# Two gated layers on one core: chunk loop outside or slice loop outside

## The chip, the cores and the metric

The kernel runs on one core of a Trainium2 chip. The metric is the time of one execution in microseconds (us), as the device measures it; the engines named below are PE (matrix products), DVE (vector), ACT (activations), POOL (a second elementwise engine) and SP (which issues the transfers). Less is better.

## The reference

The first part is an attention over 16 heads (batch 2, 8 heads, 768 positions, 64 wide) in which a query sees only the keys of its own hash bucket. Its output is 1536 tokens of 512 values, and two layers follow:

```
gate = 1.0 / (1.0 + np.exp(-(x @ w_gate)))     # 512 x 1536
val = x @ w_val                                # 512 x 1536
x = gate * val @ w_out                         # 1536 x 512
h = x @ w_in                                   # 512 x 2048
g = h * np.cos(h)
return (g @ w_out).astype(np.float32)          # 2048 x 512
```

## The kernel before

The weights come from memory as 64-bit floats. `load_raw` brings one block (128 of the 512 rows' columns, or 128 rows of 512; 512 KB) into one of three raw buffers, on SP's queue. `convert` makes 32-bit floats of it: one copy on ACT (line 150, tile `wp`) and three operations on DVE (lines 152, 155 and 169; tiles `wl`, then `w_g`, `w_v`, `w_o`, `w_i`, `w_z`). Every operand of a product is split in a high and a low part (`split`, lines 122 and 123: a cast on ACT, a subtraction on DVE or POOL), and each product is three matmuls: high by high, high by low, low by high.

The tokens are in three chunks of 512 (`xy[c]`, high and low). The inner dimension is cut in slices of 128: 12 in layer 1 (weights g, v, o), 16 in layer 2 (weights i, z). For a chunk and a slice, layer 1 does 24 matmuls in (`glu_in`) and 12 out (`layer_out1`); layer 2 does 12 in (`cos_in`) and 12 out (`layer_out2`). The inner values (`g`) go from PSUM over ACT and DVE into the buffer, are split (`gh`, `gl`), and the out matmuls add them up in four PSUM banks `a`, which are free again after a chunk.

The loop over chunks is outside:

```
units = [(1, c, f) for c in range(NC) for f in range(F1)]
units += [(2, c, f) for c in range(NC) for f in range(F2)]
```

so all weights of a layer are converted during one chunk (those of layer 1 in its first chunk, those of layer 2 during the last chunk of layer 1) and stay in the buffer as 32-bit values; the split of a weight is made anew for each chunk, 204 times in all, nearly always with POOL for the low part. There are 68 conversions. Six weights are converted already during the end of the attention.

The attention's order is written by hand. The order of the two layers on each engine's queue is made by a planner from the program text: it takes what its own clock holds to be ready, the earlier text first. An engine then works its queue strictly in that order. The last pair of heads writes the last 128 of the 512 rows of `xy[1]` and `xy[2]` (lines 454, 470 and 474); `xy[0]` is finished long before.

Of the kernel before, what the change touches and what calls it, by code (L numbers as in the profile page):

```python
# [9 lines left out]
F32 = mybir.dt.float32  # L10
F32R = mybir.dt.float32r
# [7 lines left out]
P = 128  # L19
# [20 lines left out]
def lsh_attention_glu_moe_cos_moe(  # L40
# [32 lines left out]
    OLAG = 2  # L73
    AHEAD = 9
    NFRONT = 6
# [54 lines left out]
    def load_raw(key):  # L130
        nm, f = key
# [12 lines left out]
    def convert(key):  # L144
        nm, f = key
# [17 lines left out]
        slot = order.index(key) % (3 * F1)  # L163
        if slot < NEARLY:
            w = wraw.tile([P, 512], F32, tag="we", name=f"w_{nm}{f}", bufs=NEARLY)
        else:
            pool = wf["front" if slot < NEARLY + NFRONT else "back"]
            w = pool.tile([P, 512], F32, tag="w", name=f"w_{nm}{f}")
# [10 lines left out]
    def keys(l, f):  # L179
        return [(n, f) for n in (("g", "v", "o") if l == 1 else ("i", "z"))]  # L180
# [6 lines left out]
    wf = {}  # L187

# [420 lines left out]
    def moe():  # L609
        with ExitStack() as st:  # L610
            wsp = st.enter_context(tc.tile_pool(name="wsp", bufs=2))
            wk = st.enter_context(tc.tile_pool(name="wk", bufs=2))
            wf["front"] = st.enter_context(tc.tile_pool(name="wff", bufs=NFRONT))
            wk2 = st.enter_context(tc.tile_pool(name="wk2", bufs=2))
            wf["back"] = st.enter_context(
                tc.tile_pool(name="wfb", bufs=3 * F1 - NEARLY - NFRONT)
            )
# [5 lines left out]
            def l_first(key):  # L623
                return key in (("g", 0), ("g", 1), ("v", 1))

            def wsplit(c, key):
                nm, f = key
                h = wsp.tile([P, KT, P], F32R, tag=ROLE[nm] + "h", name=f"{nm}h{c}_{f}")
                lw = wsp.tile([P, KT, P], F32R, tag=ROLE[nm] + "l", name=f"{nm}l{c}_{f}")
                sub = nc.vector if c == 0 and l_first(key) else nc.gpsimd  # L630
                split(h, lw, wt[key].rearrange("p (k c) -> p k c", k=KT), sub)
                ws[c, key] = (h, lw)

            def proj_in(ps, c, key):
                wh, wl = ws.pop((c, key))
# [8 lines left out]
            def gsplit(nm, g):  # L644
                gh = wk.tile([P, 512], F32R, tag="gh", name=f"gh{nm}", bufs=4)
                gl = wk.tile([P, 512], F32R, tag="gl", name=f"gl{nm}", bufs=4)
                split(gh, gl, g, nc.vector)
                return gh, gl

            def glu_in(c, f):  # L650
                pg = ps_h.tile([P, 512], F32, tag="h", name=f"pg{c}_{f}")
                pv_ = ps_h.tile([P, 512], F32, tag="h", name=f"pv{c}_{f}")
                proj_in(pg, c, ("g", f))
                proj_in(pv_, c, ("v", f))
                sg = wk.tile([P, 512], F32, tag="n", name=f"sg{c}_{f}")
                nc.scalar.activation(sg, pg, AF.Sigmoid)  # L656
                g = wk.tile([P, 512], F32, tag="g", name=f"g{c}_{f}")
                nc.vector.tensor_tensor(out=g, in0=pv_, in1=sg, op=ALU.mult)  # L658
                return gsplit(f"1_{c}_{f}", g)

            def cos_in(c, f):
                ph = ps_h.tile([P, 512], F32, tag="h", name=f"ph{c}_{f}")
                proj_in(ph, c, ("i", f))
# [9 lines left out]
                g = wk.tile([P, 512], F32, tag="g", name=f"g2{c}_{f}")  # L673
                nc.vector.tensor_tensor(out=g, in0=ph, in1=r, op=ALU.mult)
                return gsplit(f"2_{c}_{f}", g)
# [3 lines left out]
            def layer_out1(c, f, g):  # L679
                gh, gl = g  # L680
                wh, wl = ws.pop((c, ("o", f)))
                for e in range(KT):
                    if f == 0:
                        acc[e] = ps_a.tile([P, 512], F32, tag=f"a{e}", name=f"a1_{c}_{e}")
                    n = 0
                    for w, m in ((wh, gh), (wh, gl), (wl, gh)):
                        nc.tensor.matmul(  # L687
                            acc[e],
# [6 lines left out]
                    if f == F1 - 1:  # L695
                        nc.scalar.copy(xy[c][:, 0, e, :], acc[e])
                        nc.vector.tensor_tensor(
                            out=xy[c][:, 1, e, :],
                            in0=acc[e],
# [4 lines left out]
            def layer_out2(c, f, g):  # L704
                gh, gl = g
                wh, wl = ws.pop((c, ("z", f)))
                wh, wl = (x.rearrange("p k c -> p (k c)") for x in (wh, wl))
                for t in range(4):
                    if f == 0:
                        acc[t] = ps_a.tile([P, 512], F32, tag=f"a{t}", name=f"a2_{c}_{t}")  # L710
                    n = 0
                    ts = slice(t * P, (t + 1) * P)
                    for m, w in ((gh, wh), (gh, wl), (gl, wh)):
                        nc.tensor.matmul(  # L714
                            acc[t],
# [6 lines left out]
                    if f == F2 - 1:  # L722
                        o = wk2.tile([P, 512], F32, tag="o", name=f"o{c}_{t}", bufs=4)
                        (nc.scalar.copy if t % 2 else nc.vector.tensor_copy)(o, acc[t])
# [5 lines left out]
            units = [(1, c, f) for c in range(NC) for f in range(F1)]  # L730
            units += [(2, c, f) for c in range(NC) for f in range(F2)]

            def wsplit_for(n):
                if n < len(units):
                    l, c, f = units[n]
                    for nm in "gv" if l == 1 else "i":
                        wsplit(c, (nm, f))
                if n >= OLAG:
                    l, c, f = units[n - OLAG]
                    wsplit(c, ("o" if l == 1 else "z", f))  # L740

            pend = []
            convert_to(2 * OLAG)
            wsplit_for(0)
            for n, u in enumerate(units):
                l, c, f = u
                if l == 1:
                    if c == 0:
                        convert_to(min(3 * f + AHEAD, 3 * F1))
                    elif c == NC - 1:  # L750
                        convert_to(3 * F1 + 2 + 3 * max(0, f - 3))
                else:
                    if c == 0:
# [3 lines left out]
                if len(pend) > 2 and n != len(units) - 2:  # L757
                    (l0, c0, f0), g = pend.pop(0)
                    (layer_out1 if l0 == 1 else layer_out2)(c0, f0, g)
            wsplit_for(len(units) + 1)  # L760
            for (l0, c0, f0), g in pend:
                layer_out2(c0, f0, g)
# [44 lines left out]
```

## Time and profile before

| | |
|---|---|
| median of 3 runs | 850.98 us (847.41 to 854.46) |
| profiled execution | 848.18 us, of which the span 846.4 us |
| PE busy | 804.8 us (95%) |
| DVE, ACT, POOL busy | 594.3, 517.1, 471.5 us |
| mean granted clock of PE | 0.990 |

The span runs from the first to the last instruction; 1.8 us of the execution lie around it. Matmuls overlap in the records (each takes 0.39 us, one starts every 0.23 us), so a busy PE isn't always one at its full rate. In lists of waits, the engine and the tile that waited stand first, and then what released them.

### The profile page before, as it was taken

The numbers are of one execution on the slowest core, as the hardware profiler recorded it, in microseconds if no ns is written. First come the engines' busy times: TensorE is split into PE (matmuls) and PEld (weight loads), VectorE is DVE, ScalarE is ACT, GpSimd is POOL, SyncE is SP. The second block draws the span as 40 slices with busy tenths as digits, with TensorE's granted clock in tenths as the row PEclk, the third lists the DMA queues.
The fourth block names the chain that finished last, engine by engine and source line by source line (L and its number), as shares of the span: only waits on it lengthen the run. The fifth ranks groups of instructions, "written<-read, shape, count | busy, mean of one in ns | idle before, by whom it ended". The sixth has DMA issues, their size and how long they took to land.

```text
span 846.4 us, 12255 instructions
## 1 busy us (share of the span) xinstructions
PE 804.8 (95%) x3984; PEld 675.4 (80%) x3984; DVE 594.3 (70%) x1069; ACT 517.1 (61%) x973; POOL 471.5 (56%) x431
## 2 busy tenths in 40 slices
PE   3999999999989998899999999889999999999998
PEld 2798898898988775678888877678888888888886
DVE  4899999999999999933123797775554554455553
ACT  2798898988997454554334454447555655555553
POOL 1779788879853644474444443446444444444441
PEclk8899999999999999999999999999999999999999
DMA  8665665665524456510001354520000100000001
GB/s 197 161 154 137 150 168 139 161 169 136 137 94 141 157 165 187 189 35 1 1 0 50 125 165 142 167 74 1 1 1 0 50 2 0 1 23 28 0 1 50
DMA packets 65455, 75.38 MB, mean 89 GB/s; under 512 B 29168, under 2 KB 51696, under 8 KB 65392
## 3 DMA queue, kind: packets, MB, share of 16 engines
q1 hardware_dynamic: 65392, 74.60, 31.8%
q8 instruction: 32, 0.52, 0.3%
q14 instruction: 31, 0.25, 0.1%
HBM read 45.09 MB, written 3.15 MB: 57 GB/s over the span
## 4 chain that ended last, share of the span: by engine, by line
PE 64%; DVE 13%; issue 7%; DMA 6%; POOL 4%; ACT 4%; SPq 1%; POOLq 0%; DVEq 0%; ACTq 0%
PE a L714 15%; PE ph L639 15%; PE a L687 7%; PE pv L639 6%; PE pg L639 6%; PE t L411 4%; DVE pl L421 2%; PE s L359 2%; PE s L362 2%; PE o L432 2%; PE o L431 2%; DMA raw_z<-in_moe_w_out 2%; POOL p L402 1%; DMA raw_o<-in_moe_w_out 1%; POOL gl L123 1%
## 5 line engine op out<-in xcount | busy, mean ns | idle before, releaser
L123 DVE TENSOR_TENSOR gl<-g,gh 128x512 fp32r<-128x512 f32 x84 | 94.4, 1124 | 44.8 <-ACT gh L122 44.7
L639 PE MATMUL ph<-xy,ih 128*128 128x512 f32 x384 | 118.2, 389 | 0.0
L123 POOL TENSOR_TENSOR zl<-w_z,zh 128x512 fp32r<-128x512 f32 x48 | 62.1, 1293 | 86.2 <-ACT zh L122 83.8
L385 ACT ACTIVATE p<-s,cb 128x768 f32<-128x768 f32 x96 | 96.0, 1000 | 20.3 <-DVE cb L371 13.9
L411 PE MATMUL t<-ident,p 128*128 128x128 f32 x576 | 95.1, 273 | 3.3 <-DVE pl L421 2.3
L639 PE MATMUL pv<-xy,vh 128*128 128x512 f32 x288 | 90.8, 396 | 7.8 <-DVE g L658 4.8
L421 DVE TENSOR_TENSOR pl<-t,ph 128x384 fp32r<-128x384 f32 x192 | 96.9, 540 | 1.7 <-ACT ph L416 0.4
L416 ACT CAST ph<-t 128x384 fp32r<-128x384 f32 x192 | 90.7, 484 | 11.9 <-PE t L411 8.7
L402 POOL TENSOR_SCALAR p<-p,r 128x768 f32<-128x768 f32 x96 | 86.8, 908 | 15.4 <-DVE r L398 8.4
L366 DVE TENSOR_REDUCE mm<-s 128x1 f32<-128x768 f32 x96 | 90.6, 944 | 5.2 <-PE s L362 5.2
L123 POOL TENSOR_TENSOR il<-w_i,ih 128x512 fp32r<-128x512 f32 x48 | 62.1, 1295 | 53.1 <-ACT ih L122 53.1
L639 PE MATMUL pg<-xy,gh 128*128 128x512 f32 x288 | 89.8, 391 | 1.4 <-ACT sg L656 1.2
L411 PEld LDWEIGHTS t<-ident,p 128*128 128x128 f32 x576 | 73.7, 141 | 15.1 <-DVE pl L421 7.1
L639 PEld LDWEIGHTS ph<-xy,ih 128*128 128x128 f32 x384 | 72.1, 188 | 15.0
L123 POOL TENSOR_TENSOR ol<-w_o,oh 128x512 fp32r<-128x512 f32 x36 | 51.3, 1425 | 55.0 <-ACT oh L122 52.6
L431 PE MATMUL o<-ph,vs 128*128 128x384 f32 x192 | 80.4, 419 | 1.3 <-ACT e L440 1.3
L123 POOL TENSOR_TENSOR vl<-w_v,vh 128x512 fp32r<-128x512 f32 x35 | 50.0, 1428 | 55.2 <-ACT vh L122 48.1
L123 POOL TENSOR_TENSOR gl<-w_g,gh 128x512 fp32r<-128x512 f32 x34 | 48.8, 1437 | 55.4 <-ACT gh L122 50.7
L359 PE MATMUL s<-k,q 96*128 96x384 f32 x192 | 69.9, 364 | 10.1 <-DMA k<-bf 8.4
L714 PE MATMUL a<-zh,gh 128*128 128x512 f32 x192 | 74.7, 389 | 0.0
L639 PE MATMUL ph<-xy,il 128*128 128x512 f32 x192 | 74.7, 389 | 0.0
L714 PE MATMUL a<-zl,gh 128*128 128x512 f32 x192 | 74.7, 389 | 0.0
(106 smaller groups left out, 1957.9 us busy)
## 6 DMA issues: line engine op xcount, KB each, us to landing
q<-x SPq DMA_DIRECT2D x47, 192.0 KB, 3.3
k<-x SPq DMA_DIRECT2D x47, 192.0 KB, 3.6
raw_i<-in_moe_w_in SPq DMA_DIRECT2D x16, 512.0 KB, 3.8
raw_z<-in_moe_w_out SPq DMA_DIRECT2D x16, 512.0 KB, 3.2
raw_g<-in_moe_w_gate SPq DMA_DIRECT2D x12, 512.0 KB, 3.8
raw_v<-in_moe_w_val SPq DMA_DIRECT2D x12, 512.0 KB, 3.7
raw_o<-in_moe_w_out SPq DMA_DIRECT2D x12, 512.0 KB, 3.3
nv<-in_v SPq DMA_DIRECT2D x8, 384.0 KB, 3.5
```

What stands on the lines that cost most here:

```text
L123: sub.tensor_tensor(out=dst_l, in0=src, in1=dst_h.bitcast(F32), op=ALU.subtract)
L359: nc.tensor.matmul(o, hh["q2"][0:96, t, :], hh["k2"][0:96, sl, :], start=True, stop=False)
L366: nc.vector.tensor_reduce(mm[:, g % NM, 1:2], s_t[g], axis=AX.XY, op=ALU.min)
L385: nc.scalar.activation(pt, s_t.pop(g), AF.Exp, bias=cb[:, 1:2], scale=cb[:, 0:1], accum_out=sm)
L402: nc.gpsimd.tensor_scalar(out=pt, in0=pt, scalar1=r_t.pop(g), scalar2=1.0, op0=ALU.mult, op1=ALU.mult)
L411: nc.tensor.transpose(pt[:, i, :], pv_[:, j * P : (j + 1) * P], ident)
L416: nc.scalar.copy(ph, pt_t[w])
L421: nc.vector.tensor_tensor(out=pl, in0=pt_t.pop(w), in1=ph_t[w].bitcast(F32), op=ALU.subtract)
L431: nc.tensor.matmul(o_t[u], vs[:, j, :], ph_t.pop(w), start=(j == 0), stop=False)
L639: nc.tensor.matmul(ps, w[:, kt, :], xy[c][:, hl, kt, :], start=(n == 0), stop=(n == 11))
L687: nc.tensor.matmul(acc[e], w[:, e, :], m, start=(f == 0 and n == 0), stop=(f == F1 - 1 and n == 2),)
L714: nc.tensor.matmul(acc[t], m[:, ts], w, start=(f == 0 and n == 0), stop=(f == F2 - 1 and n == 2),)
```

## The change

In both layers the loop over slices is outside and the three chunks inside. A new list `items` gives the order: for each slice the in matmuls of chunks 1, 2 and 3 and the out matmuls of chunk 1; the out matmuls of chunks 2 and 3 follow after the last slice, slice by slice, the last two slices of chunk 2 ahead of those of chunk 3. The inner values of chunks 2 and 3 stay unsplit in 32 new buffers (`gsp`) until then. The first two slices are mixed so that chunk 1 comes first. Chunk 2 adds up in the four banks of `ps_h`, in which the in products stand else.

A weight is split once and serves all chunks, and its converted form is given back at once; the pools that held a whole layer's weights go, and six buffers (`we`) are left. The out weights (o, z) are loaded, converted and split a second time for the out matmuls of chunks 2 and 3. So there are 96 conversions and loads instead of 68, and 96 splits of weights instead of 204. The number of matmuls (2448) and of inner values' splits (84) is the same.

```diff
-    order = []
-    for f in range(F1 + OLAG):
-        order += [(nm, f) for nm in "gv" if f < F1] + [("o", f - OLAG)] * (f >= OLAG)
-    order += [kk for f in range(F2) for kk in keys(2, f)]
+    def layer_items(l, F):
+        items = [("in", l, 0, 0), ("in", l, 1, 0), ("in", l, 0, 1), ("in", l, 0, 2), ("in", l, 1, 1)]
+        items += [("out", l, 0, 0), ("in", l, 1, 2), ("out", l, 1, 0)]
+        for f in range(2, F):
+            items += [("in", l, f, c) for c in range(NC)] + [("out", l, f, 0)]
+        for f in range(F - 2):
+            items += [("out", l, f, c) for c in range(1, NC)]
+        items += [("out", l, f, c) for c in range(1, NC) for f in (F - 2, F - 1)]
+        return items
+    items = layer_items(1, F1) + layer_items(2, F2)
+    def weights_of(item):
+        kind, l, f, c = item
+        if kind == "in":
+            return [(nm, f, 0) for nm in ("gv" if l == 1 else "i")]
+        return [("o" if l == 1 else "z", f, int(c > 0))]
+    order = list(dict.fromkeys(kk for it in items for kk in weights_of(it)))
...
+            gsp = st.enter_context(tc.tile_pool(name="gsp", bufs=(NC - 1) * F2))
...
+            def gtile(l, f, c):
+                if c == 0:
+                    return wk.tile([P, 512], F32, tag="g", name=f"g{l}_{c}_{f}")
+                return gsp.tile([P, 512], F32, tag="gs", name=f"g{l}_{c}_{f}")
...
+            def acc_tile(l, c, e):
+                if c == 1:
+                    return ps_h.tile([P, 512], F32, tag="h", name=f"a{l}_{c}_{e}")
+                return ps_a.tile([P, 512], F32, tag=f"a{e}", name=f"a{l}_{c}_{e}")
...
+            def ready_to(key):
+                nonlocal ready
+                while ready <= order.index(key):
+                    convert_to(ready + 1)
+                    wsplit(order[ready])
+                    ready += 1
+                    convert_to(min(ready + NEARLY - 2, len(order)))
+            for key in weights_of(items[0]):
+                ready_to(key)
+            for n, (kind, l, f, c) in enumerate(items):
+                late = kind == "out" and c > 0
+                for it in items[n + 1 : n + (3 if late else 4)]:
+                    for key in weights_of(it):
+                        ready_to(key)
+                for it in items[n + 1 : n + 3]:
+                    if it[0] == "out" and it[1:] in gf:
+                        gsplit(*it[1:])
+                if kind == "in":
+                    (glu_in if l == 1 else cos_in)(c, f)
                 else:
-                    if c == 0:
-                        convert_to(3 * F1 + 2 * (f + 3))
-                wsplit_for(n + 1)
-                pend.append((u, glu_in(c, f) if l == 1 else cos_in(c, f)))
+                    (layer_out1 if l == 1 else layer_out2)(c, f)
```

## Rows read from the trace of the kernel before

**Rows 1.** The page: engines' busy time, and busy tenths in 40 slices.
```profile
PE 804.8 (95%) x3984; PEld 675.4 (80%) x3984; DVE 594.3 (70%) x1069; ACT 517.1 (61%) x973; POOL 471.5 (56%) x431
...
PE   3999999999989998899999999889999999999998
...
DVE  4899999999999999933123797775554554455553
```

**Rows 2.** Busy time by stretch: PE, PEld, DVE, ACT, POOL, clock, DMA share, GB/s.
```profile
600.00:830.00 230.00, 230.00 (x1017) 190.44 (x1016) 118.42 (x132) 131.97 (x215) 108.68 (x84) 1.00 0.03 10
470.00:570.00 100.00, 93.14 (x394) 73.71 (x393) 80.82 (x106) 45.25 (x80) 44.81 (x30) 0.98 0.44 138
290.00:369.00 79.00, 70.06 (x288) 52.19 (x288) 72.88 (x94) 40.93 (x71) 36.91 (x26) 1.00 0.55 171
369.00:450.00 81.00, 81.00 (x359) 67.08 (x358) 19.29 (x26) 32.55 (x56) 43.54 (x34) 1.00 0.00 1
```

**Rows 3.** The chain in order of time, its last piece: start, length, what.
```profile
831.66 10.89 PE a L714 x48
```

**Rows 4.** List of waits, 470 to 570 us: total, times, longest.
```profile
ACT wp_z L150 <- DMA raw_z<-in_moe_w_out: 21.2, 12, 4.3
...
POOL vl L123 <- ACT vh L122: 20.0, 7, 6.3
```

**Rows 5.** Timeline of ACT, 518 to 570 us: start, length, instruction, idle before.
```profile
547.95 0.68 ACT L150 ACTIVATE wp_z<-raw_z 128x512 f32<-128x512 f32 x1 [3.28 <-DMA raw_z<-in_moe_w_out]
548.52 0.62 ACT L122 CAST vh<-w_v 128x512 fp32r<-128x512 f32 x1
```

**Rows 6.** Timeline of PE, 518 to 570 us.
```profile
549.19 0.73 PE L639 MATMUL pv<-xy,vh 128*128 128x512 f32 x2 [1.69 <-ACT vh L122]
```

**Rows 7.** DVE's groups by line, 470 to 570 us: busy, mean ns, idle before.
```profile
L155 DVE SCALAR_TENSOR_TENSOR wl_i<-wp_i,wl_i 128x512 int32<-128x512 int32 x13 | 14.2, 1091 | 1.1 <-ACT wp_i L150 0.6
L155 DVE SCALAR_TENSOR_TENSOR wl_z<-wp_z,wl_z 128x512 int32<-128x512 int32 x14 | 13.4, 958 | 0.6
L169 DVE SCALAR_TENSOR_TENSOR w_i<-raw_i,wl_i 128x512 int32<-128x512 int32 x14 | 11.7, 835 | 4.1 <-POOL gl L123 2.8 <-POOL vl L123 1.2
L169 DVE SCALAR_TENSOR_TENSOR w_z<-raw_z,wl_z 128x512 int32<-128x512 int32 x14 | 10.7, 762 | 5.7 <-POOL gl L123 3.3 <-POOL vl L123 2.3
L152 DVE TENSOR_SCALAR wl_z<-raw_z 128x512 int32<-128x512 int32 x14 | 9.8, 702 | 3.0 <-DMA raw_z<-in_moe_w_out 2.9
L123 DVE TENSOR_TENSOR gl<-g,gh 128x512 fp32r<-128x512 f32 x10 | 9.0, 903 | 0.1
L152 DVE TENSOR_SCALAR wl_i<-raw_i 128x512 int32<-128x512 int32 x13 | 8.2, 628 | 4.4 <-DMA raw_i<-in_moe_w_in 4.3
```

**Rows 8.** Groups by line, whole span: DVE's work on layer 2's inner values, POOL's split.
```profile
L123 POOL TENSOR_TENSOR zl<-w_z,zh 128x512 fp32r<-128x512 f32 x48 | 62.1, 1293 | 86.2 <-ACT zh L122 83.8 <-DVE xy L697 2.4
...
L674 DVE TENSOR_TENSOR g<-ph,r 128x512 f32<-128x512 f32 x48 | 33.2, 691 | 35.6 <-ACT r L672 35.6
L669 DVE SCALAR_TENSOR_TENSOR r<-ph,n 128x512 f32<-128x512 f32 x48 | 33.2, 691 | 53.6 <-ACT n L667 53.6
```

**Rows 9.** Timeline of DVE around one operation of POOL, 517 to 520 us.
```profile
517.62 0.41 DVE L152 TENSOR_SCALAR wl_i<-raw_i 128x512 int32<-128x512 int32 x1
...
518.55 0.68 DVE L123 TENSOR_TENSOR gl<-g,gh 128x512 fp32r<-128x512 f32 x1
519.15 1.78 DVE L155 SCALAR_TENSOR_TENSOR wl_i<-wp_i,wl_i 128x512 int32<-128x512 int32 x1
```

**Rows 10.** The same stretch on POOL.
```profile
518.95 1.43 POOL L123 TENSOR_TENSOR ol<-w_o,oh 128x512 fp32r<-128x512 f32 x1 [2.40 <-ACT oh L122]
```

**Rows 11.** DMA issues of the page: number, KB each, us from issue to landing.
```profile
raw_z<-in_moe_w_out SPq DMA_DIRECT2D x16, 512.0 KB, 3.2
```

**Rows 12.** Timeline of PE at the attention's end: first matmuls of layer 1's second slice.
```profile
266.95 0.62 PE L639 MATMUL pg<-xy,gh 128*128 128x512 f32 x2
```

**Rows 13.** Timeline of POOL at the attention's end: the last rows of chunks 2 and 3.
```profile
275.37 1.33 POOL L123 TENSOR_TENSOR gl<-w_g,gh 128x512 fp32r<-128x512 f32 x1 [1.31 <-ACT gh L122]
276.67 2.30 POOL L454 TENSOR_TENSOR ef<-e,ef 128x768 f32<-128x768 f32 x1
279.48 2.70 POOL L474 TENSOR_TENSOR xy<-ef,xy 128x256 fp32r<-128x256 f32 x2 [0.52 <-ACT xy L470]
```

More of the change, by code (lines that the diff above doesn't have):

```diff
@@ L144, in convert @@
     def convert(key):
-        nm, f = key
+        nm, f, _ = key
         rw = raws.pop(key)
@@ L162, in convert @@
         )
[L163 to L168, printed above, removed]
+        w = wraw.tile([P, 512], F32, tag="we", name=f"w_{nm}{f}", bufs=NEARLY)
         nc.vector.scalar_tensor_tensor(
@@ L177, in convert @@
         wt[key] = w
-    def keys(l, f):
-        return [(n, f) for n in (("g", "v", "o") if l == 1 else ("i", "z"))]
-    order = []
-    for f in range(F1 + OLAG):
-        order += [(nm, f) for nm in "gv" if f < F1] + [("o", f - OLAG)] * (f >= OLAG)
-    order += [kk for f in range(F2) for kk in keys(2, f)]
+    def layer_items(l, F):
[7 more added lines that the diff above has]
+        return items
+    assert NC == 3
+    items = layer_items(1, F1) + layer_items(2, F2)
[5 more added lines that the diff above has]
+    order = list(dict.fromkeys(kk for it in items for kk in weights_of(it)))
     done = 0
-    wf = {}
     def convert_to(n):
@@ L621, in moe, with wsplit @@
             ws = {}
[L623 to L632, printed above, removed]
+            def wsplit(key):
+                nm, f, again = key
+                h = wsp.tile([P, KT, P], F32R, tag=ROLE[nm] + "h", name=f"{nm}h{again}_{f}")
+                lw = wsp.tile([P, KT, P], F32R, tag=ROLE[nm] + "l", name=f"{nm}l{again}_{f}")
+                sub = nc.vector if key in (("g", 0, 0), ("g", 1, 0), ("v", 1, 0)) else nc.gpsimd
+                split(h, lw, wt.pop(key).rearrange("p (k c) -> p k c", k=KT), sub)
+                ws[key] = (h, lw)
             def proj_in(ps, c, key):
-                wh, wl = ws.pop((c, key))
+                wh, wl = ws[key]
                 n = 0
@@ L642, in proj_in, with gsplit @@
                         n += 1
[L644 to L648, printed above, removed]
+            def gtile(l, f, c):
+                if c == 0:
+                    return wk.tile([P, 512], F32, tag="g", name=f"g{l}_{c}_{f}")
+                return gsp.tile([P, 512], F32, tag="gs", name=f"g{l}_{c}_{f}")
+            gf, gs = {}, {}
+            def gsplit(l, f, c):
+                gh = wk.tile([P, 512], F32R, tag="gh", name=f"gh{l}_{c}_{f}", bufs=4)
+                gl = wk.tile([P, 512], F32R, tag="gl", name=f"gl{l}_{c}_{f}", bufs=4)
+                split(gh, gl, gf.pop((l, f, c)), nc.vector)
+                gs[l, f, c] = gh, gl
             def glu_in(c, f):
@@ L695, in layer_out1 @@
                     if f == F1 - 1:
-                        nc.scalar.copy(xy[c][:, 0, e, :], acc[e])
+                        nc.scalar.copy(xy[c][:, 0, e, :], acc[c, e])
                         nc.vector.tensor_tensor(
                             out=xy[c][:, 1, e, :],
-                            in0=acc[e],
+                            in0=acc[c, e],
                             in1=xy[c][:, 0, e, :].bitcast(F32),
@@ L723, in layer_out2 @@
                         o = wk2.tile([P, 512], F32, tag="o", name=f"o{c}_{t}", bufs=4)
-                        (nc.scalar.copy if t % 2 else nc.vector.tensor_copy)(o, acc[t])
+                        (nc.scalar.copy if t % 2 else nc.vector.tensor_copy)(o, acc[c, t])
                         b, tt = divmod(4 * c + t, T)
@@ L728, in layer_out2 @@
                         )
[L730 to L740, printed above, removed]
@@ L760, in moe @@
-            wsplit_for(len(units) + 1)
-            for (l0, c0, f0), g in pend:
-                layer_out2(c0, f0, g)
+            ready = 0
+            def ready_to(key):
[7 more added lines that the diff above has]
+                ready_to(key)
```

56 lines of the change are left out of this document (18 added, 38 removed).

## The prediction, made before the changed kernel ran

> **What bounds the kernel now.** I read the page's first two parts first. PE is busy for 95% of the span, so at first sight there is little to win; but after the attention its digits fall below nine in two places (the slices from 317 and from 529 us), and DVE's are nine and seven there [rows 1]. So I asked for those stretches by themselves, with the number of matmuls in each [rows 2]. From 600 to 830 us PE starts 1017 matmuls in 230 us and from 369 to 450 us 359 in 81 us: one every 0.226 us, its full rate. From 290 to 369 us, in layer 1's first chunk, it starts only 288; at the full rate (0.2267 us, the 10.89 us of the last 48 [rows 3] divided by 48) they would have taken 65.3 of the 79 us, so 13.7 us are lost. From 470 to 570 us, in layer 1's last chunk, it starts 394, which need 89.3 of 100 us: 10.7 us are lost. Together that is 24.4 us. PE's idle time in the same rows is 8.9 and 6.9 us, 15.8 in all. I take the count: where each matmul waits a little for its weights, the records stretch and hide the wait. The Trainium skill ("Perfetto Trace Analysis", Identifying the Most-Contended Engine) says the same of matmul busy time, that it is no measure of PE's headroom because matmuls are pipelined; by the busy time the gain would be 15.8 us, by the count 24.4, and the weight loads agree with the count (74% busy from 470 to 570 us, 83% from 600 on).
>
> What the two stretches have in common is that nearly all weights are loaded and converted there: three weights for every 36 matmuls of layer 1, which last 36 x 0.2267 = 8.16 us. From 290 to 369 us DVE is busy for 72.9 of 79 us: it is the bound itself. From 470 to 570 us it is 80.8%, and the wait that ends last is another. ACT's copy of a raw weight waits for the transfer 12 times, 21.2 us in all (the other weight of layer 2 has as much again), and POOL's split of v waits 20.0 us for its cast [rows 4]. One instance: ACT sits 3.28 us for a raw z, and only then casts v [rows 5], for which PE has by then waited 1.69 us [rows 6]. With three raw buffers, 3.2 us from issue to landing [rows 11] and DVE's work behind it, a weight every 2.7 us (8.16 / 3) is more than the ring gives.
>
> **The change part by part.** *The rate at which weights are wanted.* Layer 1 now needs three weights for 72 + 12 = 84 matmuls (19.0 us), layer 2 two for 48 (10.9 us), and the second pass over o and z one for 24 (5.44 us). That is one in 5.4 to 6.3 us, half of what the two bad stretches ask. A raw buffer comes round every three weights, so every 16 us, against 3.2 us of transfer: the ACT wait of [rows 4] should go. The 28 extra loads (14.7 MB) lie in this; two in 10.9 us are 96 GB/s where 171 were moved [rows 2].
>
> *DVE.* A conversion takes 0.63 + 1.09 + 0.84 = 2.55 us for i and 0.70 + 0.96 + 0.76 = 2.42 us for z [rows 7]. The tightest stretch is layer 2's slices: two conversions 4.98, three times r and g at 0.69 each [rows 8] 4.15, one low part 0.90 [rows 7]: 10.0 us of 10.9. But these durations are from a stretch where POOL is busy for 45% [rows 2], and they hang on POOL: alone the operations take 0.41 and 0.68 us, and the one that meets POOL's split takes 1.78 and ends with it [rows 9, 10]. At 0.41 + 0.68 + 0.68 for a conversion and 0.68 for the low part a slice needs 8.4 us. POOL will do two splits of 1.29 us [rows 8] in 10.9 us, 24%; in proportion that gives 8.4 + (10.0 - 8.4) x 24/45 = 9.3 us. I take 9.3, with 8.4 and 10.0 as ends; all are under 10.9, so DVE isn't the bound. The Trainium skill ("SBUF — State Buffer", Who interferes with whom) speaks against this middle: DVE and POOL have a port pair under an exclusive lock, and the later one blocks fully. If both splits of a slice block DVE for their whole 1.29 us, the slice needs 8.4 + 2.6 = 11.0 us, and 16 slices would lose 1 to 2 us; the pair at 1.78 us agrees with the lock.
>
> Layer 1's slices need three conversions (7.5 us), three g and one low part, 10.5 of 19.0 us. The second pass needs one conversion and two low parts, 4.2 of 5.44 us, behind which only the next out matmuls stand; they have two items of lead.
>
> *POOL and ACT.* POOL loses 108 of 204 weight splits at 1.29 us or more, some 140 us of work, and ACT as many casts against 28 more copies. POOL's split of an out weight is wanted 5.44 us after it is set going. Neither is on the path.
>
> *PE.* 2448 matmuls before and after, so nothing. What goes is the waiting: 24.4 us.
>
> *The start.* Chunks 2 and 3 are now wanted at once. The second slice's products begin at 266.95 us [rows 12]; its 24 matmuls for chunk 1 and the attention's last ones end near 273. Then chunk 2's in matmuls: 9 of them read rows that are long there, until 275; the tenth needs the last quarter, which POOL finishes from 279.5 to 282.2 us [rows 13]. If PE's queue is in the order of the text, PE waits until about 281, so 6 us. If the planner puts the second product's first 9 matmuls, those of chunk 3 and the ready out matmuls in front, it has 27 x 0.2267 = 6.1 us and more to fill the hole with, and waits for nothing. POOL may also be earlier: the sum that comes before started behind a split of 1.33 us [rows 13], and fewer splits are due now. Ends 0 and 6; I take 2, nearer to nothing, as before the layers' matmuls already fill the attention's last gaps.
>
> *The turns.* At the first out matmuls of chunk 2 four banks of `ps_h` have to be empty. The last in product goes through n, r, the sine and g, some 2.8 us if each is about 0.7 as r and g are [rows 8]; ahead of the last bank lie 12 + 9 matmuls, 4.8 us. Between the layers two in items of chunk 1 lie ahead of the first use of a new `xy[1]`. The tail after the last matmul is the same four copies and transfers. For these, and for single late weights or inner values, no row shows a price; the nearest are the single waits of 1.7 us on PE [rows 6], and there are four turns: 0 to 7 us, I take 1.5, since each has cover.
>
> *The sum*, against the profiled execution: 848.2 - 24.4 + 2 + 1.5 = 827.3 us. The three runs have a median 2.8 us above that execution and lie over 7 us; I add half of the 2.8 and predict 829 us.
>
> **The rivals.** *Per weight, not per rate (slower).* PE may stop a moment for each converted weight, however slowly they come, because ACT and DVE work strictly in the planner's order and its clock differs from the chip's. From 470 to 570 us 27 weights cost 10.7 us, 0.40 us each. Then the 90 weights after the first six cost 36 us in place of 24.4: 848.2 - 24.4 + 36 + 1.4 = 861 us. It decides the sign from 0.27 us per weight on (24.4 / 90). Against it: from 470 us on the wait is for transfers, which will have 16 us. Chance 0.08.
>
> *DVE's own waiting in layer 2 (same).* r waits 53.6 us for 48 n and g 35.6 us for the sine [rows 8], 1.9 us for each in item, in a stretch where DVE has nothing else to do. Three such in a slice are 5.6 us on top of 9.3, and only 1.6 are free. If conversions fill all but half, a slice takes 9.3 + 2.8 = 12.1 us, 16 x 1.2 = 19 us more: 848 us. For it: conversions would have to sit just in those holes. Against it: from 290 to 369 us DVE is 92% busy, so the planner fills such holes well. Chance 0.09.
>
> *The planner doesn't follow the text (same).* It may draw conversions or later slices forward so far that the rate stays uneven. The six `we` buffers and the two split buffers per kind forbid most of that. About 851 us, chance 0.03.
>
> **How the numbers follow.** The forecast has 0.80, with its own range of 822 (no wait at the start or the turns: 823.8, less the spread) to 840 (6 and 7 us there, 836.8, and 3 for DVE at its upper end). About 1% is what a measurement of this kernel can tell from no change; all of the forecast's range is beyond it. So faster 0.80, same 0.12 from the two milder rivals, slower 0.08 from the first. The upper end at 845 takes in half of the second rival.
>
> **What would show it.** PE starts 44 matmuls in each 10 us from 290 us to the end, and its digits are nine throughout; ACT's waits for raw z and i are gone; POOL falls to about a quarter and DVE stays near 85% in layer 2's slices and 50 to 60% in layer 1's; a gap of PE between 273 and 282 us shows the start's price, and gaps at the four turns theirs. It is wrong if PE waits for `vh`, `ih` or `zh` all along (the first rival), if `ph` waits for a bank that g holds (the second), or if PE's clock falls after a long wait at the start.

## The result and the profile after

The changed kernel takes 841.88 us (median of 4 runs, 840.57 to 843.6) against 851.63 us for the kernel before on the same chip: a ratio of 0.9891, 95% interval 0.9844 to 0.9938. The sign of the forecast holds, its size doesn't: some 10 us are gained where 22 were forecast (and 5.6 us in a second measurement, e5_after_again). The profiled execution took 840.57 us (span 838.8 us), 7.6 us less than the profiled execution of before.

The page's first two parts after the change answer to [rows 1]:

```profile
PE 802.3 (96%) x3984; PEld 673.3 (80%) x3984; DVE 580.6 (69%) x1153; ACT 471.3 (56%) x893; POOL 325.3 (39%) x323
...
PE   3899999999989999999999999999999999999998
...
```

PE's digits are nine nearly throughout, POOL has fallen from 471.5 to 325.3 us, and behind the attention no engine but PE looks full. By this part nothing is left to gain. As before the change, the number of matmuls by stretch tells more. Here are four stretches of the kernel after, one behind the other (columns as in [rows 2]: PE, PEld, DVE, ACT, POOL, clock, DMA share, GB/s):

```profile
258.00:290.00 32.00, 30.22 (x138) 24.38 (x137) 31.11 (x45) 17.27 (x30) 10.59 (x7) 1.00 0.58 178
290.00:580.00 290.00, 289.43 (x1277) 239.32 (x1276) 155.62 (x236) 109.75 (x188) 64.89 (x47) 1.00 0.28 87
580.00:746.00 166.00, 156.33 (x659) 121.15 (x658) 110.94 (x176) 93.32 (x152) 35.86 (x26) 1.00 0.26 86
746.00:830.00 84.00, 83.97 (x371) 69.21 (x370) 39.66 (x62) 33.65 (x58) 19.39 (x15) 1.00 0.15 54
```

At 0.2267 us each, the 1277 matmuls from 290 to 580 us need 289.5 of 290 us, the 371 from 746 us on need 84.1 of 84 us: layer 1 and layer 2's second pass run at PE's full rate. From 580 to 746 us, in layer 2's slices, 659 need 149.4 of 166 us: **16.6 us are lost** there. Before the change this layer's stretch was the full one (1017 matmuls in 230 us, [rows 2]). So the loss of 24.4 us is gone from where it was, and two thirds of it have come back elsewhere.

The list of waits from 580 to 746 us (total us, times, longest) has many short ones and no large one on the path:

```profile
...
ACT wp_z L147 <- DMA raw_z<-in_moe_w_out: 23.6, 15, 2.5
DVE g L681 <- ACT r L679: 16.7, 28, 0.8
...
DVE w_i L161 <- POOL il L120: 10.6, 9, 1.2
PE a L726 <- ACT gh L119: 9.7, 13, 1.4
DVE gl L120 <- ACT gh L119: 9.1, 7, 1.7
DVE w_z L161 <- POOL zl L120: 7.5, 7, 1.5
...
DVE wl_z L149 <- DMA raw_z<-in_moe_w_out: 4.9, 8, 1.0
ACT wp_i L147 <- DMA raw_i<-in_moe_w_in: 4.2, 4, 1.2
DVE w_z L161 <- POOL il L120: 3.5, 3, 1.2
...
```

PE waits 13 times, about once in a slice, and always for the cast `gh` of chunk 1's inner value. DVE's six groups of waits make 52.3 us, with two of 0.4 us 53.1; its work is 110.9 us. Together that is 164.0 of 166 us, though its share of busy time is 67%. The sum by itself proves nothing: an engine that isn't busy is nearly always in some wait (e9_no_convert below has work and waits that fill the stretch too, with PE at its full rate). What DVE waits for tells more: of the 53.1 us, 21.6 are for POOL's splits and 4.9 for a transfer, all ahead of steps of a conversion. Divided by 659 / 48 = 13.7 slices, a slice is 8.1 us of DVE's work, 3.9 us of its waiting, and 12.1 us in all, where PE needs 10.9.

Waits of this kind need not cost anything: from 290 to 580 us ACT waits 38.3, 18.4 and 16.5 us for raw o, g and v, and PE is full there, with 19.0 us for a slice of layer 1. One instance in layer 2, on the timelines of POOL, DVE, ACT and PE (start, length, instruction, idle before), shows what stands ahead of `gh`:

```profile
613.23 1.30 POOL L120 TENSOR_TENSOR il<-w_i,ih 128x512 fp32r<-128x512 f32 x1 [7.25 <-ACT ih L119]
```

```profile
614.56 0.69 DVE L161 SCALAR_TENSOR_TENSOR w_i<-raw_i,wl_i 128x512 int32<-128x512 int32 x1 [1.19 <-POOL il L120]
```

```profile
619.59 0.68 ACT L147 ACTIVATE wp_z<-raw_z 128x512 f32<-128x512 f32 x1 [2.47 <-DMA raw_z<-in_moe_w_out]
620.18 0.67 ACT L674 ACTIVATE n<-ph,quarter 128x512 int32<-128x512 f32 x1
...
623.09 0.66 ACT L147 ACTIVATE wp_i<-raw_i 128x512 f32<-128x512 f32 x1 [0.74 <-DMA raw_i<-in_moe_w_in]
623.65 0.60 ACT L119 CAST gh<-g 128x512 fp32r<-128x512 f32 x1
```

```profile
624.31 0.50 PE L726 MATMUL a<-zh,gh 128*128 128x512 f32 x1 [1.42 <-ACT gh L119]
```

ACT stands 2.47 us before a raw z that PE wants only some weights later; chunk 1's `n` is queued behind it, then follow `r`, the sine, `g`, another copy of a raw weight with its own 0.74 us, and only then `gh`. DVE has stood 1.19 us before `w_i`, whose buffer POOL's split was still reading, with chunk 3's `r` of the slice before behind it (615.17 us). The chain of waits one slice later, in order of time (start, length, what), joins the links:

```profile
627.51 1.31 POOL il L120
...
628.84 0.70 DVE w_i L161
...
629.56 3.24 DMA raw_z<-in_moe_w_out
...
632.89 0.43 DVE wl_z L149
633.32 0.61 DVE r L676
...
634.71 0.70 DVE g L681
...
635.44 0.63 ACT gh L119
...
636.11 3.29 PE a L726 x12
```

POOL's split frees a buffer of `we`, DVE fills it and with that frees a raw buffer, the transfer fills that in 3.24 us, and DVE's first step on it stands ahead of `r`, the sine, `g` and `gh`. Each link starts as soon as the one before ends. That reads as if the conversions ran as far ahead as the buffers let them, with the inner value that PE wants next waiting behind them; the experiments test it.

The start, on PE's timeline, answers to [rows 12]:

```profile
266.97 0.45 PE L438 MATMUL o<-pl,vs 128*128 128x384 f32 x1 [0.29 <-DVE pl L427]
...
269.26 0.50 PE L639 MATMUL pv<-xy,vl 128*128 128x512 f32 x1 [0.93 <-DVE vl L120]
...
275.57 0.50 PE L639 MATMUL pg<-xy,gh 128*128 128x512 f32 x1 [0.57 <-POOL xy L480]
```

and on POOL's, to [rows 13]:

```profile
274.28 2.94 POOL L480 TENSOR_TENSOR xy<-ef,xy 128x256 fp32r<-128x256 f32 x2 [0.52 <-ACT xy L476]
```

POOL comes to the last rows of `xy` 5.2 us earlier (274.28 against 279.48), and PE's two waits make 1.5 us. The attention's last matmul begins at 266.97 us; before, it was this row:

```profile
269.73 0.45 PE L432 MATMUL o<-pl,vs 128*128 128x384 f32 x1 [0.32 <-DVE pl L421]
```

### The profile page after: what moved, and what is told of

Same layout as the page of the kernel before. It is cut to its first block, busy times and chain, and to the rows that moved or that the text cites. A ratio compares the mean times of both kernels' runs of the same rounds, so it can differ in the third digit from the quotient of the medians.

```text
span 838.8 us, 12103 instructions
## 1 busy us (share of the span) xinstructions
PE 802.3 (96%) x3984; PEld 673.3 (80%) x3984; DVE 580.6 (69%) x1153; ACT 471.3 (56%) x893; POOL 325.3 (39%) x323
## 4 chain that ended last, share of the span: by engine, by line
PE 66%; issue 11%; DVE 8%; DMA 6%; ACT 5%; POOL 3%; SPq 1%; POOLq 0%; DVEq 0%; ACTq 0%
PE a L726 14%; PE a L699 11%; PE pg L639 10%; PE pv L639 10%; PE ph L639 5%; PE t L417 5%; DMA raw_z<-in_moe_w_out 3%; PE s L365 2%; PE s L368 2%; PE o L438 2%; PE o L437 2%; DVE pl L427 2%; PE pb L326 1%; ACT p L391 1%; DMA e<-e 1%
## 5 line engine op out<-in xcount | busy, mean ns | idle before, releaser
L120 DVE TENSOR_TENSOR gl<-g,gh 128x512 fp32r<-128x512 f32 x84 | 66.4, 797 | 69.7 <-ACT gh L119 68.4
L422 ACT CAST ph<-t 128x384 fp32r<-128x384 f32 x192 | 90.7, 485 | 11.7 <-PE t L417 8.6
L372 DVE TENSOR_REDUCE mm<-s 128x1 f32<-128x768 f32 x96 | 90.7, 945 | 4.0 <-PE s L368 4.0
L639 PE MATMUL pv<-xy,vh 128*128 128x512 f32 x288 | 89.0, 389 | 0.0
L120 POOL TENSOR_TENSOR zl<-w_z,zh 128x512 fp32r<-128x512 f32 x32 | 43.6, 1363 | 110.5 <-ACT zh L119 110.5
L119 ACT CAST gh<-g 128x512 fp32r<-128x512 f32 x84 | 51.4, 617 | 52.7 <-PE a L726 44.5
L726 PE MATMUL a<-zh,gl 128*128 128x512 f32 x192 | 76.3, 397 | 0.0
L120 POOL TENSOR_TENSOR ol<-w_o,oh 128x512 fp32r<-128x512 f32 x24 | 32.5, 1353 | 110.5 <-ACT oh L119 107.5
L438 PE MATMUL o<-pl,vs 128*128 128x384 f32 x192 | 65.4, 341 | 1.5 <-DVE pl L427 1.5
```

The lines of the kernel that those rows point to most:

```text
L120: sub.tensor_tensor(out=dst_l, in0=src, in1=dst_h.bitcast(F32), op=ALU.subtract)
L372: nc.vector.tensor_reduce(mm[:, g % NM, 1:2], s_t[g], axis=AX.XY, op=ALU.min)
L422: nc.scalar.copy(ph, pt_t[w])
L639: nc.tensor.matmul(ps, w[:, kt, :], xy[c][:, hl, kt, :], start=(n == 0), stop=(n == 11))
L726: nc.tensor.matmul(acc[c, t], m[:, ts], w, start=(f == 0 and n == 0), stop=(f == F2 - 1 and n == 2),)
```

## Experiments

The question is what takes 17 us in layer 2's slices. Theory A: ACT's waits for raw weights. B: chunk 1's inner value has too short a lead, so that any delay of it reaches PE. C: DVE can't do a slice's work in 10.9 us. D, which followed C after four runs: DVE has too much work beside what it must wait for. The last, E, came out of the first eight runs: the order of the queues; the planner puts every step of a conversion as far forward as its own clock and the buffers allow.

The stage is measured on PE's timeline, from the first `ph` matmul to the last: 755 matmuls, 171.2 us at the full rate. "Rest" is from there to the last matmul (89.8 us at the full rate). Ratios are to the kernel before on the same chip.

| run | median us | ratio [95%] | slices us | rest us |
|---|---|---|---|---|
| after (profiled once) | 841.88 | 0.9891 [0.9844, 0.9938] | 188.3 | 90.1 |
| e1_raw4 | 844.89 | 0.992 [0.989, 0.995] | 188.9 | 90.6 |
| e2_lag | 847.47 | 0.9965 [0.9947, 0.9982] | 187.0 | 95.7 |
| e3_wpool | 859.2 | 1.0097 [1.0061, 1.0134] | 182.2 | 90.6 |
| e4_dve_more | 852.83 | 1.0024 [1.0005, 1.0043] | 197.1 | 90.3 |
| e5_after_again | 843.94 | 0.9937 [0.992, 0.9953] | 187.8 | 90.1 |
| e6_gl_pool | 845.09 | 0.9947 [0.9928, 0.9967] | 188.4 | 90.2 |
| e7_dve_less | 847.03 | 0.9964 [0.9946, 0.9982] | 191.7 | 90.7 |
| e8_we7 | 842.28 | 0.9911 [0.9889, 0.9932] | 187.6 | 89.8 |
| e9_no_convert | 824.7 | 0.9687 [0.9664, 0.9709] | 171.1 | 89.8 |
| e10_anchor | 829.75 | 0.9742 [0.9725, 0.976] | 174.9 | 89.9 |
| e11_anchor_dve | 831.72 | 0.9773 [0.9749, 0.9797] | 178.7 | 89.9 |
| e12_anchor_lag | 838.98 | 0.9847 [0.9822, 0.9872] | 175.9 | 100.1 |

**e1_raw4: a fourth raw buffer** (and one fewer for `o`, to make room).

```diff
-        rw = wraw.tile([P, 512], I64, tag="raw", name=f"raw_{nm}{f}")
+        rw = wraw.tile([P, 512], I64, tag="raw", name=f"raw_{nm}{f}", bufs=4)
...
-                load_to(done + 3)
+                load_to(done + 4)
...
-                        o = wk2.tile([P, 512], F32, tag="o", name=f"o{c}_{t}", bufs=4)
+                        o = wk2.tile([P, 512], F32, tag="o", name=f"o{c}_{t}", bufs=3)
```

> Four raw buffers instead of three, and each load issued one weight earlier (the output buffers o go from 4 to 3 to make room). Theory A (in layer 2's slices ACT stands before a raw weight that is still on its way, and n and gh of chunk 1 behind it come late): the waits of wp for raw, 27.8 us between 580 and 746 us, go nearly all, PE's loss of some 16 us there falls to under 4, and the time goes from 841 to 826 to 830 us. Theory B (the out matmuls of chunk 1 follow too closely on its in matmuls, whatever ACT waits for): the loss stays above 10 us, 835 us or more. Theory C (DVE can't do a slice's work in 10.9 us): no change, 839 to 843 us.

The slices stay (188.9 us), and so do ACT's waits for raw weights, 25.7 us in layer 2's slices:

```profile
ACT wp_i L147 <- DMA raw_i<-in_moe_w_in: 14.6, 7, 2.3
ACT wp_z L147 <- DMA raw_z<-in_moe_w_out: 11.1, 11, 1.6
```

A third more of buffers did not take the wait away. A isn't refuted by this, since the wait is still there; the time, 844.89 us, is in the range given for B and 2 us above C's.

**e2_lag: layer 1's and 2's out products of chunk 1 one in product later**, behind the next slice's first.

```diff
-            items += [("in", l, f, c) for c in range(NC)] + [("out", l, f, 0)]
+            items += [("in", l, f, 0)] + [("out", l, f - 1, 0)] * (f > 2)
+            items += [("in", l, f, c) for c in range(1, NC)]
+        items += [("out", l, F - 1, 0)]
```

> From the third slice on the out matmuls of chunk 1 stand behind the next slice's first in product, 2.7 us later for layer 2; the rest as it is. PE's longest single wait for gh is 1.4 us now. A and B: the lead covers the late gh, PE's waits in layer 2's slices go, 825 to 830 us, while under A ACT goes on waiting for raw weights for 20 us or more. C: DVE has the same work in the same time, the waits come back at another place, 838 us or more.

ACT's waits for raw weights are down to 2.7 us, and the slices are as long (187.0 us); other waits have taken the place:

```profile
...
DVE w_z L161 <- POOL il L120: 14.3, 12, 1.2
...
PE a L728 <- DVE gl L120: 6.6, 10, 0.7
...
ACT wp_i L147 <- DMA raw_i<-in_moe_w_in: 1.6, 2, 1.4
ACT wp_z L147 <- DMA raw_z<-in_moe_w_out: 1.1, 3, 0.6
```

In this order neither the waits for transfers nor the lead of one inner value sets the length of a slice, against what A and B had; the whole, 847.47 us, is in C's range (838 or more, the waits at another place). What is late now is the low part `gl`, whose step on DVE takes 1.31 us on the mean against 0.69 in after. The turn behind the slices costs 5 us more (rest 95.7).

**e3_wpool: the copy `wp` on POOL in place of ACT.**

```diff
-        nc.scalar.mul(pt, hw.bitcast(F32), float(2.0**-112))
+        nc.gpsimd.tensor_scalar(
+            out=pt, in0=hw.bitcast(F32), scalar1=float(2.0**-112), scalar2=1.0, op0=ALU.mult, op1=ALU.mult
+        )
```

> The copy wp of each raw weight is made by POOL instead of ACT, for all 96 weights. A: ACT waits for no transfer any more, gh of chunk 1 is in time, 826 to 832 us (POOL's waits for transfers now stand before the weight splits, which have more lead; some stalls may come from there). B: 833 us or more. C: POOL's extra 96 operations lock DVE out for longer, 845 us or more.

The slices shorten by 6.1 us, to 182.2, so ACT's place in A has a part in them. But POOL now waits for transfers ahead of its splits, 24.9 us for raw o alone from 400 to 580 us, and layer 1's second pass waits for `ol`: layer 1, from the attention's last matmul to the first `ph`, takes 302.1 us against 289.3 (266.97 to 556.29). The attention's last matmul, too, begins 10.8 us later (277.81 us); what delays it is open. So the kernel is slower than before, 859.2 us, which fits B's and C's ranges alike: moving the wait to another engine moves the loss.

**e4_dve_more: one step of the conversions of i and z twice on DVE.**

```diff
-        nc.vector.tensor_scalar(
-            out=lt, in0=lw, scalar1=29, scalar2=7, op0=ALU.logical_shift_right, op1=ALU.bitwise_and
-        )
+        for _ in range(2 if nm in "iz" else 1):
+            nc.vector.tensor_scalar(
+                out=lt, in0=lw, scalar1=29, scalar2=7, op0=ALU.logical_shift_right, op1=ALU.bitwise_and
+            )
```

> The first DVE operation of each conversion of layer 2's weights (shift and mask, 0.4 to 0.5 us) is made twice: 48 operations, some 22 us more on DVE, 0.9 us in each slice. A and B: DVE has room, 840 to 845 us. C: in the 16 slices each 0.9 us more comes out as time, 14 us, and more in the second pass: 853 us or more.

DVE works 132.1 us from 583 to 755 us, in which PE starts 646 matmuls: 9.8 us for a slice's 48, against 8.1 in after. The slices grow by 8.8 us, 0.55 us each: a third of the added 1.7, so most of the added work fills former waits. The 852.83 us all but reach C's range (853 or more), but its 14 us in the slices didn't come.

**e5_after_again: the changed kernel once more**, unchanged, beside the next three.

> The changed kernel as it is, as a yardstick on the chip of the next runs. 840 to 846 us; layer 2's slices (first to last ph) last 187 to 190 us, where 755 matmuls at full rate need 171.

Ratio 0.9937 [0.992, 0.9953], within the interval of the first measurement, if at its end: 5.6 us are gained in this one. The slices take 187.8 us, and DVE's work from 583 to 745 us is 108.7 us, with 51.2 us of waits.

**e6_gl_pool: the low part `gl` of chunk 1 in layer 2 on POOL**, 0.69 us of DVE's work in a slice less.

```diff
-                split(gh, gl, gf.pop((l, f, c)), nc.vector)
+                split(gh, gl, gf.pop((l, f, c)), nc.gpsimd if l == 2 and c == 0 else nc.vector)
```

> In layer 2 the low part of chunk 1's inner values (gl, once in a slice) is made by POOL instead of DVE. Theory D (DVE works its queue in order, and its work of some 8 us in a slice plus its waits at the head of the queue of some 4 us make 12 us, over the 10.9 that PE needs): DVE gets rid of 0.7 us of work and 0.5 us of waiting for gh, the slices go from 188 to 170 to 177 us and the whole from 841 to 826 to 833. Theory A (ACT's waits for raw weights): no change. Theory B (too little lead): the low part takes 1.3 us instead of 0.7 and comes later, slices 190 us or more.

DVE works 100.2 us from 583 to 745 us, 8.5 less than in e5_after_again, and the slices take 188.4 us where D had 170 to 177: nothing gained. The run doesn't test D alone, though, since PE now waits for the low part, which POOL brings later:

```profile
PE a L726 <- POOL gl L120: 7.9, 13, 0.6
```

**e7_dve_less: two steps of DVE in place of three for each i and z.**

```diff
+        if nm in "iz":
+            nc.vector.tensor_scalar(
+                out=lt, in0=pt.bitcast(I32), scalar1=3, scalar2=0, op0=ALU.logical_shift_left, op1=ALU.bitwise_or
+            )
+        else:
...
```

> The conversion of layer 2's weights leaves out the three lowest bits of the fraction: one DVE operation (a shift) instead of two, some 0.6 us less for each of 48 weights, 1.2 us less in a slice, and nothing else is moved. D: slices from 188 to 171 to 178 us, the whole 826 to 834 us. A and B: DVE isn't on the path, slices 185 us or more.

This leaves out part of the computation, the three lowest bits of a weight's fraction. DVE's work falls to 91.4 us and the slices don't shorten (191.7 us, where D had 171 to 178). The stage of this run, by stretch and by waits:

```profile
583.00:745.00 162.00, 150.44 (x626) 116.32 (x625) 91.43 (x143) 89.05 (x145) 36.00 (x25) 0.99 0.28 88
```

```profile
DVE gl L120 <- ACT gh L119: 22.0, 12, 2.3
...
DVE g L686 <- ACT r L684: 15.3, 28, 0.8
DVE wl_z L150 <- ACT wp_z L147: 14.8, 11, 2.2
...
DVE w_i L166 <- POOL il L120: 10.5, 9, 1.2
```

Neither C nor D gets its shorter slices: 17 us of work went against e5_after_again, and DVE's waits took its place, 69.3 us in all (62.6 in the four groups shown) against 51.2 in the same stretch. One of the new ones, 14.8 us for ACT's copy, comes with the edit: the first of the two steps left reads that copy and no longer the raw weight.

**e8_we7: seven `we` buffers in place of six.**

```diff
-        w = wraw.tile([P, 512], F32, tag="we", name=f"w_{nm}{f}", bufs=NEARLY)
+        w = wraw.tile([P, 512], F32, tag="we", name=f"w_{nm}{f}", bufs=NEARLY + 1)
```

> Seven buffers for converted weights instead of six. If DVE's waits for POOL (21 us in the slices) come from too few buffers, they go and the slices fall to 175 us or less. If the planner fills any number of buffers as soon as it can, the seventh is filled too, the waits stay within 16 to 26 us and the slices at 185 to 190 us; this is what D expects.

```profile
DVE w_z L161 <- POOL il L120: 14.1, 12, 1.2
...
DVE w_i L161 <- POOL zl L120: 5.2, 5, 1.2
```

With another 3.5 us DVE's waits for POOL's splits are 22.8 us where after has 21.6. With six buffers it was mostly the i that waited for a split of i and the z for one of z, now it is the z for i and the i for z: one weight further on in the ring, as it must be if the buffer is the cause. So the planner fills seven as it fills six, as had been expected for that case.

**e9_no_convert: layer 2's weights converted and loaded for the first slice alone** and used for all.

```diff
+        if nm in "iz" and f > 0 or nm == "z" and key[2]:
+            return
...
+        if nm in first:
+            wt[key] = first[nm]
+            return
...
+        if nm in "iz":
+            w = first[nm] = wraw.tile([P, 512], F32, tag="w0" + nm, name=f"w_{nm}{f}", bufs=1)
+        else:
+            w = wraw.tile([P, 512], F32, tag="we", name=f"w_{nm}{f}", bufs=NEARLY - 1)
```

> Leaves out part of the computation: in layer 2 only the first slice's i and z are loaded and converted, and their converted values serve all slices; all splits, casts and matmuls stay. Theory E (the planner puts each conversion as far forward as its own clock and the buffers allow, so the conversion's steps stand at the head of ACT's and DVE's queues and wait there for a transfer or for POOL, with n, r, the sine, g and gh of the out matmuls behind them): without conversions the slices (first to last ph) fall from 188 to 171 to 174 us. Theory B (the lead of chunk 1's out matmuls is too short in any case): 180 us or more. The whole 822 to 832 us.

```profile
584.00:729.00 145.00, 145.00 (x642) 120.05 (x641) 62.94 (x93) 77.45 (x118) 32.49 (x26) 1.00 0.00 1
```

PE is at its full rate. The casts and POOL's splits of the weights are still there (26 on POOL, as after), and so are n, r, the sine, g and the low part: without the conversions these fit. All of the 17 us belong to the conversions, with their loads, which are gone here too. DVE's work of 62.9 us and its waits fill these 145 us as well. `g` waits 23.9 us for the sine, and `r` for n:

```profile
DVE r L686 <- ACT n L684: 59.6, 40, 3.3
```

ACT's n in turn waits for PE's `ph` (37.1 us). So a full sum of work and waits doesn't show that an engine holds PE up: here it is PE that DVE waits for in the end.

**e10_anchor: the conversions held back.** Nothing of a conversion is queued on an engine ahead of the latest sine and the latest g that the text has come to; work, buffers and items are the changed kernel's. (The planner also put one more matmul ahead of the first with a low part.)

```diff
-            convert(order[done])
+            with ExitStack() as queued:
+                for ins in behind.values():
+                    queued.enter_context(tc.issue_after(ins))
+                convert(order[done])
...
-                nc.scalar.activation(r, r, AF.Sin, bias=halfpi, scale=TWOPI)
+                behind["act"] = nc.scalar.activation(r, r, AF.Sin, bias=halfpi, scale=TWOPI).ins
...
-                nc.vector.tensor_tensor(out=g, in0=ph, in1=r, op=ALU.mult)
+                behind["dve"] = nc.vector.tensor_tensor(out=g, in0=ph, in1=r, op=ALU.mult).ins
```

> All the work of the changed kernel, but in layer 2 each conversion's steps are queued on ACT and DVE behind the sine and the g that stand ahead of it in the text, so the planner can't put them further forward. E: DVE's waits for POOL's split and ACT's for raw weights (21 and 28 us in the slices) fall to a few us, the slices to 171 to 177 us, the whole to 826 to 834 us. If the planner's order has nothing to do with it: slices 185 us or more, 840 us or more.

829.75 us, ratio 0.9742 [0.9725, 0.976]: faster than both kernels, and as E had it (826 to 834). The slices take 174.9 us, 13.4 less, of the 17.1 that could be had. The stage by stretch and by waits:

```profile
583.00:732.00 149.00, 147.80 (x642) 119.29 (x642) 121.26 (x175) 89.90 (x147) 34.10 (x26) 1.00 0.30 97
```

```profile
ACT n L679 <- PE ph L644: 27.0, 14, 2.1
DVE g L686 <- ACT r L684: 21.4, 27, 0.8
...
PE a L731 <- DVE gl L120: 1.2, 2, 1.0
```

No wait for a transfer is left on ACT, none for POOL on DVE, and PE waits 1.2 us in place of 9.7. ACT's wait for PE's `ph` has grown from 11.1 to 27.0 us: it is done early and PE sets the pace. What the list of waits does not show is that a meeting with POOL still costs something. On DVE's timeline the step of z is long, and on POOL's the split of z starts with it:

```profile
649.89 1.83 DVE L152 SCALAR_TENSOR_TENSOR wl_z<-wp_z,wl_z 128x512 int32<-128x512 int32 x1
```

```profile
649.88 1.29 POOL L120 TENSOR_TENSOR zl<-w_z,zh 128x512 fp32r<-128x512 f32 x1 [1.84 <-ACT zh L119]
```

DVE's work is therefore 121.3 us here, 9.1 us for a slice's 48 matmuls against 8.1 in after, and PE still gains 13 us, so the amount of DVE's work (C) isn't what sets the slices' length: what counts is where the lost time of DVE stands in the queue.

**e11_anchor_dve: only behind the g.** As e10_anchor, without the line of the sine.

> The same, with only DVE's steps of the conversions held behind g; ACT's copies wp go where the planner likes. E with the waits for POOL as the larger part: slices 171 to 178 us. If ACT's waits for raw weights are the larger part: 182 us or more.

Slices 178.7 us, 9.6 less than after and just above the range given for the waits for POOL as the larger part (171 to 178). On ACT the copies are again ahead, and wait for DVE 15 times, 25.7 us in all.

**e12_anchor_lag: e10_anchor with e2_lag's order of the items.**

> Both: conversions of layer 2 held behind on ACT and DVE, and the out matmuls of chunk 1 one in product later. If the order is the whole cause, the lead adds nothing: within 3 us of the run with held conversions alone. If some of the lead is wanted as well, 3 us or more below it.

Slices 175.9 us, no better than e10_anchor's 174.9: the longer lead brings nothing there either. The whole, 838.98 us, is 9.2 us above e10_anchor's, which neither expectation had, because its turn costs 10 us (rest 100.1). Two stretches of 5 us at the turn:

```profile
745.00:750.00 5.00, 1.53 (x7) 0.94 (x5) 4.31 (x9) 2.12 (x4) 5.00 (x1) 0.96 0.52 165
750.00:755.00 5.00, 4.52 (x11) 3.55 (x12) 2.35 (x2) 0.00 (x0) 1.66 (x2) 0.50 0.42 149
```

PE waits 2.56 us for a low part (to 737.80 us) and 3.95 us for POOL's split of z (to 750.48 us), and the clock falls behind that.

## Why the prediction was wrong, point by point

**Right: the old loss goes.** All of the 24.4 us in [rows 2] are gone: 290 to 580 us is full. Layer 1's conversions and the second pass with its 28 extra loads are hidden; DVE is busy 156 of 290 us there, 54%, as forecast. PE has no wait per weight in layer 1, and in layer 2's slices it waits for no weight: that rival falls. Its reason, that ACT and DVE work strictly in the planner's order, comes back in the slices, with the inner value as what is late.

**Right in size: start and turns.** I had put 2 + 1.5 us. The accounts against the two profiled executions are 848.2 - 24.4 + 16.6 (slices) - 2.8 (the attention ends 2.8 us earlier, which I had not counted) = 837.6; 840.6 were measured, so 3.0 us are left for start and turns. Of these the rows show 0.93 + 0.57 = 1.5 us at the start. Part of the 2.8 us is spread: in e5_after_again, the same kernel, the attention's last matmul begins at 268.48 us, 1.5 us later. POOL's fall (146 us, forecast some 140) and ACT's (46 us) are as told, and POOL's earlier arrival at `xy` was the cover that I had named as possible.

**Wrong: the slices of layer 2, 16.6 us where I had nothing.** Two sentences of the prediction failed, for one reason. The first is "A raw buffer comes round every three weights, so every 16 us, against 3.2 us of transfer: the ACT wait of [rows 4] should go". The conclusion is false, whatever the time of a round: that a ring has 16 us for a round gives ACT no slack if the planner queues each copy ahead of work that is wanted sooner. The waits were 23.6 + 4.2 us in the stage. The second is "all are under 10.9, so DVE isn't the bound". My 9.3 us of work in a slice were even too many (8.1 measured, 67% busy where I had expected 85%; DVE meets POOL here mostly in waits for a buffer, 21.6 us, and less in the long operations that I priced). But work against time of a stage is a test of an engine that may run its work at any time. DVE runs it in the queue's order, and a step of a conversion that stands at the head and waits for POOL or a transfer holds up the `r`, `g` and `gl` behind it. One reading beside that sum doesn't hold either: the step of 1.78 us in [rows 9] doesn't end with POOL's split in [rows 10] but 0.55 us behind it (520.93 against 520.38).

The rival "DVE's own waiting in layer 2" had the place and the price (a slice of 12.1 us, 19 us in all; measured 12.0 by the stage and 17), and I gave it 0.09. That the price fits is in part luck: its work was 1.2 us too high and its waits 1.1 us too low (2.8 against 3.9). The sign that I had named for it, `ph` waiting for a bank that g holds, didn't show: all 13 waits of PE in the stage are for `gh`. I argued against it that the planner fills DVE's holes well. It fills them, with conversions, and that is the harm: what fills a hole of n or the sine can itself be a step that waits for POOL, for a transfer or for ACT. The waits that make up the 3.9 us are not only those of r and g which that rival named (16.7 of 53.1 us), but those of the conversions and of `gh` as well.

The 841.88 us lie above the 840 that my sum gave as the forecast's upper end. They are below the 845 that I then named as an upper end, but that took in half of this rival; no term of the sum reaches there.

**What shows the cause.** The conversions with their loads take it all (e9_no_convert: full rate without them). None of these changes gives it back by itself: less work on DVE (e7_dve_less; e6_gl_pool says less, as it makes the low part later), one more raw buffer (e1_raw4), one more `we` buffer (e8_we7), ACT freed of its waits for transfers (e2_lag: same slices; e3_wpool: 6.1 us), a longer lead of the inner value (e2_lag, e12_anchor_lag). The same conversions with the same buffers, behind the inner values and not ahead of them, give back 13.4 of 17.1 us (e10_anchor); with DVE's place alone, 9.6 (e11_anchor_dve). So for these 13.4 us it is the order in the queues.

The Trainium skill ("SBUF — State Buffer", Who interferes with whom) has an exclusive lock on a pair of ports that DVE and POOL share. e10_anchor's step of 1.83 us beside a split of 1.29 agrees with the lock. My estimate of 11.0 us for a slice with both splits blocking DVE is close to e10_anchor's slice of 174.9 x 48 / 755 = 11.1 us only by chance: there the split of z alone meets a long step, and DVE's work is 9.1 us in a slice.

e10_anchor comes within 1 us of my 829, by luck, with other terms than mine: its slices still lose 3.7 us, and layer 2 begins 3 us later than in the changed kernel (559.26 against 556.29 us). On PE's timeline 3 of the 3.7 us stand at the first matmul with a low part: two waits for `gl` (1.5 us, by the starts) and 13 gaps of 0.1 us (1.5 us) right behind it. Why `gl` is late twice is open; DVE's work and waits are 143.6 of 149 us there, and 21.4 of its 22.3 us of waits are for the sine.

## What to carry to other kernels

Where a planner orders the queues, spare time in a ring of buffers or on an engine need not be slack for the work on the path: look in the timeline at which steps stand at the head of each in-order queue, what they wait for, and what stands behind them. An engine at 67% isn't free if its waits are for a buffer or a transfer ahead of wanted work; if they end at the engine that is full, as in e9_no_convert, they cost nothing. If taking one wait away lets another grow by as much, as here, try the order before widening resources: hold the work that can wait behind the latest work that is wanted. Price a rival by the same sum as the forecast, and ask of "the planner fills such holes" what it fills them with.

## What had not been expected of the hardware

- One step of DVE, `wl_z<-wp_z,wl_z` on 128x512, takes 0.69 us on the mean in the changed kernel's slices and 1.61 us in e10_anchor's (16 of them, 25.8 us), with the same operands: 13 of the 16 take 1.82 or 1.83 us, and in the instance above POOL's split starts with it. In the changed kernel DVE stood 1.19 us before `w_i` behind a split of 1.30 us instead. So an operation's mean time in one order doesn't give its cost in another.
- PE's granted clock fell behind PE's waits within the layers. In e12_anchor_lag's turn PE started 7 matmuls from 745 to 750 us; from 750 to 755 us the granted clock was 0.50, its lower level of 1.2 GHz, and PE, busy for 4.52 of 5 us, started only 11. From 760 to 765 us it was 1.00, 2.4 GHz, again. Shorter waits were enough at e10_anchor's start: behind 1.00 and 0.81 us with one matmul between them, the clock is 0.81 on the mean from 275 to 280 us. The changed kernel, whose waits at the start were 0.93 and 0.57 us, kept 1.00 from 258 to 290 us.
